# Values and row sums of two head pairs in one stretch of 32-column tiles, in an attention and GELU kernel

## The chip, the cores and the metric

The kernel runs on one core of one Trainium2 chip. The metric is the device time of one execution in microseconds (us). The engines are named as in the profile: PE is TensorE's matmul side and PEld its loading of weights, DVE is VectorE, ACT is ScalarE, POOL is GpSimd, SP is the engine that issues most DMAs.

## The reference

Cosine attention over 8 batches of 12 heads (448 positions of 64 elements), then a layer of two matrices with an exact GELU between them over all 3584 positions.

```python
q_n = q / (norm(q) + 1e-06)
k_n = k / (norm(k) + 1e-06)
scores = q_n @ k_n.transpose(0, 1, 3, 2) / tau
attn = exp(scores - max(scores))
attn = attn / (sum(attn) + 1e-09)
x = (attn @ v), heads side by side          # 3584 x 768
h = x @ w_in                                # 768 x 2048
out = (0.5 * h * (1 + erf(h / sqrt(2)))) @ w_out    # 2048 x 768
```

## The kernel before

A batch has six pairs of heads; a pair's two heads fill the 128 partitions of a tile (64 each). With normalised q and k the scores are bounded, so no maximum is subtracted. The kernel goes through the batches in turn: an attention stage `attention(b, fill)` of six intervals, then a linear stage `first(b)` with the first matrix and the GELU. The second matrix's matmuls (`second_pieces`, 128 rows by 384 columns, 16 of them to an output tile) are cut into single matmuls and put as filling, `run(n)`, between the pieces of the next attention stage. A batch pair has seven blocks of 128 rows: batches 1, 3, 5 and 7 get three blocks, which is 96 filling matmuls, and batches 2, 4 and 6 get four, which is 128. Batch 0 has its own attention code with nothing to fill in.

A pair's scores come in four chunks of 112 keys; TensorE writes a chunk for both heads, ScalarE makes exp of it:

```python
def scores(g, c0):
    qkT = qkT_t[g]
    for c in (c0, c0 + 1):
        st = ps_st.tile([128, 2, 512], F32, tag="st")        # 2 buffers
        for h in range(2):
            rows = slice(h * D, (h + 1) * D)
            nc.tensor.matmul(st[:CS, h, :S], lhsT=qkT[rows, 1, c, :], rhs=qkT[rows, 0, :, :], ...)
        pt = ptp.tile([CS, 2, S], BF16, tag="pt")            # 12 buffers
        nc.scalar.activation(pt, st[:CS, :, :S], AF.Exp, scale=inv_tau)
```

The values, the row sums and the division. `o` and `sm` have one PSUM buffer each. The sums of two pairs (four heads) are made by `sums_two` as four tiles of 32 columns side by side, turned into reciprocals on VectorE, and spread over the partitions through a DMA to memory and back; `sums_one` makes those of one pair with 64 columns each, so that they need no DMA:

```python
def values(g, copy):
    o = ps_acc.tile([128, 512], F32, tag="o")                # 1 buffer
    for c in range(NC):
        for h in range(2):
            nc.tensor.matmul(o[h * D:(h + 1) * D, :S], lhsT=v_t[g][:, h, c, :],
                             rhs=pt_t[g, c][:, h, :], start=(c == 0), stop=(c == NC - 1))
    os_t[g] = o[:, :S]
    if copy:
        os = osp.tile([128, S], F32, tag="os")
        nc.vector.tensor_copy(os, o[:, :S])
        os_t[g] = os

def sums_two(g):
    sm = ps_acc.tile([128, 512], F32, tag="sm")              # 1 buffer
    for c in range(NC):
        for j in range(2):
            for h in range(2):
                r = 32 * (2 * j + h)
                nc.tensor.matmul(sm[r:r + 32, :S], lhsT=ones[:, :32], rhs=pt_t[g + j, c][:, h, :],
                                 start=(c == 0), stop=(c == NC - 1), tile_position=(0, r))
    rs = reciprocal(g, sm)               # VectorE: transpose (tr), reciprocal (rc), transpose (rs)
    nc.sync.dma_start(out=rows[g:g + 2]..., in_=rs[0:128:32, :])
    rb = osp.tile([128, 2, S], F32, tag="rb", bufs=2)
    for h in range(2):
        nc.sync.dma_start(out=rb[h * D:(h + 1) * D], in_=rows[g:g + 2, h, :].partition_broadcast(D))
    # ... rb_t[g + j] = rb[:, j, :]; the exp tiles are dropped

def normalise(g, eng):
    eng.tensor_tensor(x_t[b][:, p, :], os_t.pop(g), rb_t.pop(g), ALU.mult)
```

The attention stage. The calls `upto(f, n)` issue the steps f of later pairs up to number n: scaling (`scale`, GpSimd) and transposing (`transposes`, DMA) of this batch's q and k, squares (GpSimd) and their sums (`reduce`, VectorE) and loads for the next:

```python
def attention(b, fill):
    # ... run(n) issues the next n filling matmuls
    tail = 12
    nxt = (b + 1) * HP
    for i in range(HP):
        g = b * HP + i
        share = (len(fill) - tail) // (HP - i)
        if i > 0:
            scores(g, 0)
        # ... roots, scale, transposes of this batch
        upto(square, nxt + min(i, 3))
        upto(reduce, nxt + min(max(i - 1, 0), 3))
        one = i == HP - 1
        if i == 0:
            run(24)
        else:
            run(share // 3)
            if one:
                sums_one(g - 1)
            values(g - 1, not one)
            if i in (2, 4):
                sums_two(g - 2)
        scores(g, 2)
        if one:
            normalise(g - 1, nc.vector)
        if i in (0, 3):
            upto(load_v, g // 3 + 3, NV)
        if i in (3, 5):
            for j in (3, 2):
                normalise(g - j, nc.gpsimd)
        if i in (3, 4):
            upto(load_qk, nxt + i + 2)
        run(share - share // 3 if i else 6)
    g = b * HP + HP - 1
    run(len(fill))
    sums_one(g)
    values(g, False)
    normalise(g, nc.vector)
```

The linear stage takes the pairs of x in the order 0, 1, 4, 2, 3 and 5 (batch 0: as they come), as pairs 2 and 3 wait for the DMA of their sums; the first scores of the next batch end it:

```python
def first(b):
    # ... for each of 16 output blocks m: 6 matmuls hp <- x, wi (128 x 448), then GELU on ScalarE
    upto(load_wo, 4)
    for n in range(nxt + 1, nxt + 4):
        upto(scale, n)
        upto(transposes, n)
    upto(load_qk, nxt + 10)
    upto(square, nxt + 6)
    upto(reduce, nxt + 6)
    # ...
    scores(nxt, 0)
```

Of the kernel before, what the change touches and what calls it, by code (L numbers as in the profile page):

```python
# [15 lines left out]
def kernel(  # L16
# [15 lines left out]
    nc = tc.nc  # L32
    B, H, S, D = q.shape
    NC = 4
    CS = S // NC
    HP = H // 2
# [52 lines left out]
    qk_t, v_t, sq_t, nq_t, rn_t, qkb_t, qkT_t, pt_t = {}, {}, {}, {}, {}, {}, {}, {}  # L89
# [96 lines left out]
# [3 lines that stand above are left out]
            st = ps_st.tile([128, 2, 512], F32, tag="st", name=f"st{g}_{c}")  # L189
            for h in range(2):  # L190
                rows = slice(h * D, (h + 1) * D)
                nc.tensor.matmul(st[:CS, h, :S], lhsT=qkT[rows, 1, c, :], rhs=qkT[rows, 0, :, :],  # L192
                                 start=True, stop=True)
            pt = ptp.tile([CS, 2, S], BF16, tag="pt", name=f"pt{g}_{c}")
            nc.scalar.activation(pt, st[:CS, :, :S], AF.Exp, scale=inv_tau)  # L195
            pt_t[g, c] = pt

    def values(g, copy):
        o = ps_acc.tile([128, 512], F32, tag="o", name=f"o{g}")
        for c in range(NC):  # L200
            for h in range(2):
                nc.tensor.matmul(o[h * D:(h + 1) * D, :S], lhsT=v_t[g][:, h, c, :],  # L202
                                 rhs=pt_t[g, c][:, h, :], start=(c == 0), stop=(c == NC - 1))
        os_t[g] = o[:, :S]
        if copy:
            os = osp.tile([128, S], F32, tag="os", name=f"os{g}")
            nc.vector.tensor_copy(os, o[:, :S])  # L207
            os_t[g] = os
        v_t.pop(g)
# [3 lines left out]
    def reciprocal(g, sm):  # L213
        tr = rcp.tile([128, S // 32, 32], F32, tag="tr", name=f"tr{g}")
        nc.vector.transpose(tr.rearrange("p b r -> p (b r)"), sm[:, :S])  # L215
        rc = rcp.tile([128, S // 32], F32, tag="rc", name=f"rc{g}")
        nc.vector.reciprocal(rc, tr[:, :, 0])
        rs = rcp.tile([128, S // 32, 32], F32, tag="rs", name=f"rs{g}")
        nc.vector.transpose(rs, rc.to_broadcast([128, S // 32, 32]))  # L219
        return rs.rearrange("p b r -> p (b r)")  # L220


    def sums_one(g):
        sm = ps_acc.tile([128, 512], F32, tag="sm", name=f"sm{g}")
        for c in range(NC):
            for h in range(2):
                nc.tensor.matmul(sm[h * D:(h + 1) * D, :S], lhsT=ones, rhs=pt_t[g, c][:, h, :],  # L227
                                 start=(c == 0), stop=(c == NC - 1))
        rb_t[g] = reciprocal(g, sm)
# [3 lines left out]
    def sums_two(g):  # L233
        sm = ps_acc.tile([128, 512], F32, tag="sm", name=f"sm{g}")
# [6 lines that stand above are left out]
        rs = reciprocal(g, sm)  # L241
        nc.sync.dma_start(out=rows[g:g + 2].rearrange("j h s -> (j h) s"), in_=rs[0:128:32, :])
        rb = osp.tile([128, 2, S], F32, tag="rb", name=f"rb{g}", bufs=2)
        for h in range(2):
            nc.sync.dma_start(out=rb[h * D:(h + 1) * D], in_=rows[g:g + 2, h, :].partition_broadcast(D))
        for j in range(2):
            rb_t[g + j] = rb[:, j, :]
            for c in range(NC):
                pt_t.pop((g + j, c))

    def normalise(g, eng):
        b, p = divmod(g, HP)
        eng.tensor_tensor(x_t[b][:, p, :], os_t.pop(g), rb_t.pop(g), ALU.mult)  # L253
# [48 lines left out]
    def upto(f, n, last=NG):  # L302
        while done.get(f, 0) < min(n, last):
            done[f] = done.get(f, 0) + 1
            f(done[f] - 1)

    def roots(n):
        upto(root, n, len(groups))
# [9 lines left out]
    def attention_first():  # L318
# [25 lines left out]
        upto(reduce, HP + 3)  # L344
        sums_one(HP - 1)
        values(HP - 1, False)
        normalise(HP - 1, nc.vector)
        upto(load_wo, 2)


    def attention(b, fill):
        fill = list(fill)

        def run(n):
            for _ in range(max(0, min(n, len(fill)))):
                fill.pop(0)()

        x_t[b] = xp.tile([128, HP, S], BF16, tag="x", name=f"x{b}")
        tail = 12
        nxt = (b + 1) * HP  # L360
        for i in range(HP):
            g = b * HP + i
            share = (len(fill) - tail) // (HP - i)
            if i > 0:
                scores(g, 0)

            if i == HP - 1:
                roots(2 * b + 7)
            upto(scale, min(g + 4, nxt))
            upto(transposes, min(g + 4, nxt))  # L370
            upto(square, nxt + min(i, 3))
            upto(reduce, nxt + min(max(i - 1, 0), 3))
            one = i == HP - 1
            if i == 0:
                run(24)
            else:
                run(share // 3)
                if one:
                    sums_one(g - 1)
                values(g - 1, not one)  # L380
                if i in (2, 4):
                    sums_two(g - 2)
            scores(g, 2)
            if one:
                normalise(g - 1, nc.vector)
            if i in (0, 3):
                upto(load_v, g // 3 + 3, NV)
            if i in (3, 5):
                for j in (3, 2):
                    normalise(g - j, nc.gpsimd)  # L390
            if i in (3, 4):
                upto(load_qk, nxt + i + 2)
            run(share - share // 3 if i else 6)
        g = b * HP + HP - 1
        run(len(fill))
        sums_one(g)
        values(g, False)
        normalise(g, nc.vector)


    def first(b):
        sb, hf = divmod(b, 2)
        if hf == 0:
            g_t[sb] = gp.tile([128, KF, 2 * S], BF16, tag="g", name=f"g{sb}")
        if b == 0:
            roots(HP + 1)
        nc.scalar.preload_act_table_set(GELU_SET)
        nxt = (b + 1) * HP
        hps = {}


        order = (0, 1, 4, 2, 3) if b else range(KD - 1)

        def mm(m, kds):
            for kd in kds:
                nc.tensor.matmul(hps[m], lhsT=wi[:, kd, m * 128:(m + 1) * 128],  # L416
                                 rhs=x_t[b][:, kd, :], start=(kd == 0), stop=(kd == KD - 1))


        for m in range(2):  # L420
            hps[m] = ps_mm.tile([128, 512], F32, tag="mm", name=f"hp{b}_{m}")[:, :S]
            mm(m, order)
        st = ps_st.tile([128, 2, 512], F32, tag="st", name=f"hp{b}_2")
        for m in range(2, 4):
            hps[m] = st[:, m - 2, :S]
            mm(m, order)
        upto(load_wo, 4)
        for n in range(nxt + 1, nxt + 4):
            upto(scale, n)
            upto(transposes, n)  # L430
        upto(load_qk, nxt + 10)
        upto(square, nxt + 6)
        upto(reduce, nxt + 6)
        for m in range(4):
            mm(m, (KD - 1,))
        for m in range(KF):
            if m > 3:
                hps[m] = ps_mm.tile([128, 512], F32, tag="mm", name=f"hp{b}_{m}")[:, :S]
                mm(m, range(KD))
            nc.scalar.activation(g_t[sb][:, m, hf * S:(hf + 1) * S], hps.pop(m), AF.Gelu)  # L440
        if b + 1 < B:
            nc.scalar.preload_act_table_set(EXP_SET)
            roots(2 * b + 8)
            scores(nxt, 0)
# [25 lines left out]
    fill = []  # L470
    for b in range(B):
        if b == 0:
            attention_first()
        else:
            attention(b, fill)
        first(b)
        sb, hf = divmod(b, 2)
        todo = [(t, ni) for t in (range(3) if hf == 0 else range(3, 7)) for ni in range(2)]
        if b == 0:
            todo.sort(key=lambda x: x[1])  # L480
        fill = [f for t, ni in todo for f in second_pieces(sb, t, ni)]
# [37 lines left out]
```

## Time and profile before

| | |
|---|---|
| time, median of three | 457.26 us (456.58 to 458.76) |
| span of the profiled execution | 456.8 us |
| TensorE busy | 443.7 us, 2912 matmuls |
| ScalarE busy | 264.7 us |
| GpSimd busy | 234.1 us |
| VectorE busy | 180.2 us |
| granted TensorE clock, mean of the span | 0.993 |
| attention stages, 96 filling matmuls (batches 1, 3, 5, 7) | 33.49, 32.24, 32.06, 32.07 us |
| attention stages, 128 filling matmuls (batches 2, 4, 6) | 36.69, 36.70, 36.70 us |

The two lower rows were read off the chain that ended last: a stage goes from the first filling matmul to the first matmul of the linear stage. A matmul's duration in the profile is that of its passage through the array, in which the next one already runs: to find what a matmul costs, take the difference between starts, not the duration. In the profile's names a line such as `o<-pt,v 112*64 112x448 bf16` is a matmul into the tile o with 112 rows and 64 columns of weights and 448 moving columns. `st` are scores, `op` is the filling (second matrix), `hp` the first matrix, `o` the values, `sm` the row sums.

### The profile page before, as it was taken

What the parts mean: (1) busy time and instruction counts of PE and PEld (TensorE: products, weight loads), DVE (VectorE), ACT (ScalarE), POOL (GpSimd) and SP (SyncE); (2) the same over time, 40 slices, a digit from 0 to 9 for tenths busy, and PEclk for the clock granted to TensorE, in tenths of its full rate; (3) what the DMA queues carried; (4) which work ended last, traced back from release to release, by engine and by line L of the source; (5) the groups of instructions that cost most, each with busy time, mean ns of one, the idle gap of its engine ahead of it and who ended that gap; (6) DMA issues with size and microseconds to landing.
All of it is one profiled execution on the core that took longest, in us unless ns stands there. A gap on an engine that the chain in (4) does not pass through costs nothing.

```text
span 456.8 us, 7314 instructions
## 1 busy us (share of the span) xinstructions
PE 443.7 (97%) x2912; PEld 216.8 (47%) x2912; DVE 180.2 (39%) x294; ACT 264.7 (58%) x380; POOL 234.1 (51%) x213
## 2 busy tenths in 40 slices
PE   7999998999999999999999999999999999999995
PEld 4444543445445554455444554445444554444563
DVE  4686316532365305443255322753054431342021
ACT  4886486636665467744767358745766357773300
POOL 3997756391934719274642928367381744121000
PEclk9899999999999999999999999999999999999998
DMA  8999999764864817757456566747185711821022
GB/s 202 238 241 207 195 209 199 199 159 113 126 145 139 198 37 128 165 132 188 61 121 177 128 160 103 148 138 188 35 131 141 181 31 19 142 84 34 1 69 70
DMA packets 87458, 61.46 MB, mean 135 GB/s; under 512 B 42312, under 2 KB 82304, under 8 KB 87424
## 3 DMA queue, kind: packets, MB, share of 16 engines
q1 hardware_dynamic: 70400, 48.97, 45.4%
q0 software_dynamic: 16784, 11.80, 17.9%
q8 instruction: 22, 0.36, 0.3%
q10 hardware_dynamic: 240, 0.23, 0.2%
q14 instruction: 12, 0.10, 0.1%
HBM read 52.04 MB, written 11.11 MB: 138 GB/s over the span
## 4 chain that ended last, share of the span: by engine, by line
PE 86%; ACT 6%; DMA 4%; POOL 1%; issue 1%; DVE 1%; SPq 0%; POOLq 0%
PE hp L416 31%; PE op L267 31%; PE st L192 9%; PE o L202 8%; ACT pt L195 5%; PE sm L227 3%; PE sm L239 2%; DMA v<-in_v_dram 2%; DMA qkT<-qkb 2%; POOL qkb L166 1%; ACT g L440 1%; PE spin L314 1%; DMA qk<-in_q_dram 1%; DVE nq L137 0%; PE tp L182 0%
## 5 line engine op out<-in xcount | busy, mean ns | idle before, releaser
L195 ACT ACTIVATE pt<-st 112x896 bf16<-112x896 f32 x192 | 164.4, 913 | 56.6 <-PE st L192 56.4
L267 PE MATMUL op<-wo,g 128*128 128x384 bf16 x896 | 160.4, 327 | 0.0
L416 PE MATMUL hp<-x,wi 128*128 128x448 bf16 x768 | 148.1, 352 | 0.5
L440 ACT ACTIVATE g<-hp 128x448 bf16<-128x448 f32 x128 | 67.0, 545 | 99.8 <-PE hp L416 99.2
L267 PEld LDWEIGHTS <-g 128*128 128x128 bf16 x896 | 80.7, 98 | 72.2 <-issue 25.0
L416 PEld LDWEIGHTS <-wi 128*128 128x128 bf16 x768 | 74.4, 98 | 73.6 <-issue 3.3
L166 POOL TENSOR_TENSOR qkb<-qk,rn 112x512 bf16<-112x512 f32 x95 | 96.8, 1046 | 7.6 <-DVE rn L157 7.4
L127 POOL TENSOR_TENSOR sq<-qk 112x1024 f32<-112x1024 f32 x44 | 82.3, 1889 | 1.7 <-DMA qk<-in_k_dram 1.6
L139 DVE TENSOR_REDUCE nq<-sq 112x16 f32<-112x1024 f32 x47 | 57.0, 1215 | 59.4 <-POOL sq L127 59.3
L253 POOL TENSOR_TENSOR x<-os,rb 128x448 bf16<-128x448 f32 x28 | 31.2, 1133 | 80.4 <-DMA rb<-rows 66.9
L192 PE MATMUL st<-qkT 64*112 64x448 bf16 x384 | 60.9, 376 | 4.3 <-ACT pt L195 1.9
L271 DVE COPY ot<-op 128x384 f32<-128x384 f32 x56 | 30.5, 545 | 85.7 <-PE op L267 85.7
L155 POOL TENSOR_SCALAR se<-sr 112x48 f32<-112x48 f32 x14 | 4.6, 327 | 84.1 <-ACT sr L154 84.1
L202 PE MATMUL o<-pt,v 112*64 112x448 bf16 x384 | 45.1, 357 | 0.4 <-DMA v<-in_v_dram 0.4
L192 PEld LDWEIGHTS <-qkT 64*112 64x112 bf16 x384 | 21.1, 125 | 42.4 <-issue 36.8
L157 DVE RECIPROCAL rn<-se 112x48 f32<-112x48 f32 (+1 forms) x20 | 7.8, 392 | 79.3 <-POOL se L155 79.0
L202 PEld LDWEIGHTS <-v 112*64 112x64 bf16 x384 | 18.9, 109 | 19.9 <-issue 9.7
L207 DVE COPY os<-o 128x448 f32<-128x448 f32 x28 | 17.5, 624 | 24.5 <-PE o L202 24.5
L215 DVE STREAM_TRANSPOSE tr<-sm 128x448 f32<-128x448 f32 x34 | 21.7, 637 | 8.4 <-PE sm L227 5.1
L219 DVE STREAM_TRANSPOSE rs<-rc 128x448 f32<-128x448 f32 x34 | 21.9, 645 | 1.2
L227 PE MATMUL sm<-pt,ones 112*64 112x448 bf16 x160 | 19.0, 359 | 0.0
L314 PE MATMUL spin<-blank,ident 112*112 112x448 bf16 x48 | 14.7, 456 | 1.3 <-POOL ident masks.py:199 1.3
(35 smaller groups left out, 124.0 us busy)
## 6 DMA issues: line engine op xcount, KB each, us to landing
qk<-in_q_dram SPq DMA_DIRECT2D x48, 224.0 KB, 4.9
qk<-in_k_dram SPq DMA_DIRECT2D x47, 224.0 KB, 5.1
rb<-rows SPq DMA_DIRECT2D x28, 224.0 KB, 4.7
v<-in_v_dram POOLq DMA_DIRECT2D x15, 336.0 KB, 5.9
wi<-in_moe_w_in_dram POOLq DMA_DIRECT2D x4, 768.0 KB, 11.6
wo<-in_moe_w_out_dram POOLq DMA_DIRECT2D x4, 768.0 KB, 18.0
out_dram<-ot SPq DMA_DIRECT2D x8, 336.0 KB
out_dram<-ot SPq DMA_DIRECT2D x8, 288.0 KB
```

What stands on the lines that cost most here:

```text
L127: nc.gpsimd.tensor_tensor(sq, t, t, ALU.mult)
L139: nc.vector.tensor_reduce(nq, sq, mybir.AxisListType.X, ALU.add)
L166: eng.tensor_tensor(qkb[:, i].rearrange("p c h d -> p h c d"), t[:, i], rn[:, i].to_broadcast([CS, 2, NC, D]), ALU.mult)
L192: nc.tensor.matmul(st[:CS, h, :S], lhsT=qkT[rows, 1, c, :], rhs=qkT[rows, 0, :, :], start=True, stop=True)
L195: nc.scalar.activation(pt, st[:CS, :, :S], AF.Exp, scale=inv_tau)
L202: nc.tensor.matmul(o[h * D:(h + 1) * D, :S], lhsT=v_t[g][:, h, c, :], rhs=pt_t[g, c][:, h, :], start=(c == 0), stop=(c == NC - 1))
L227: nc.tensor.matmul(sm[h * D:(h + 1) * D, :S], lhsT=ones, rhs=pt_t[g, c][:, h, :], start=(c == 0), stop=(c == NC - 1))
L253: eng.tensor_tensor(x_t[b][:, p, :], os_t.pop(g), rb_t.pop(g), ALU.mult)
L267: nc.tensor.matmul(ps[:, :NH], lhsT=g_t[sb][:, kf, t * 128:(t + 1) * 128], rhs=wo[:, kf, ni * NH:(ni + 1) * NH], start=(kf == 0), stop=(kf ...
L271: nc.vector.tensor_copy(ot[:, ni * NH:(ni + 1) * NH], ps[:, :NH])
L416: nc.tensor.matmul(hps[m], lhsT=wi[:, kd, m * 128:(m + 1) * 128], rhs=x_t[b][:, kd, :], start=(kd == 0), stop=(kd == KD - 1))
L440: nc.scalar.activation(g_t[sb][:, m, hf * S:(hf + 1) * S], hps.pop(m), AF.Gelu)
```

## The change

The values of the pairs 0 to 3 of a batch are computed with 32 columns of weights at a time (two matmuls for what was one), the form that the sums of two pairs have. They are held back so that two pairs' values and their four heads' sums come one after another, values, sums, values, in the intervals 2 and 4, with no matmul of another form between. The intervals 1 and 3 are left with scores and filling only, and the filling is shared out by a fixed plan in place of equal shares. The change is meant to have TensorE change its form less often. In batch 0's linear stage fewer q and k loads are issued, and the rest in the first interval of batch 1.

```diff
--- before.py
+++ after.py
@@ -197,10 +197,13 @@
 
     def values(g, copy):
         o = ps_acc.tile([128, 512], F32, tag="o", name=f"o{g}")
+        w = 32 if copy else D
         for c in range(NC):
             for h in range(2):
-                nc.tensor.matmul(o[h * D:(h + 1) * D, :S], lhsT=v_t[g][:, h, c, :],
-                                 rhs=pt_t[g, c][:, h, :], start=(c == 0), stop=(c == NC - 1))
+                for r in range(0, D, w):
+                    nc.tensor.matmul(o[h * D + r:h * D + r + w, :S], lhsT=v_t[g][:, h, c, r:r + w],
+                                     rhs=pt_t[g, c][:, h, :], start=(c == 0), stop=(c == NC - 1),
+                                     tile_position=(0, h * D + r))
         os_t[g] = o[:, :S]
         if copy:
             os = osp.tile([128, S], F32, tag="os", name=f"os{g}")
@@ -245,8 +248,6 @@
             nc.sync.dma_start(out=rb[h * D:(h + 1) * D], in_=rows[g:g + 2, h, :].partition_broadcast(D))
         for j in range(2):
             rb_t[g + j] = rb[:, j, :]
-            for c in range(NC):
-                pt_t.pop((g + j, c))
 
     def normalise(g, eng):
         b, p = divmod(g, HP)
@@ -356,11 +357,12 @@
                 fill.pop(0)()
 
         x_t[b] = xp.tile([128, HP, S], BF16, tag="x", name=f"x{b}")
-        tail = 12
         nxt = (b + 1) * HP
+
+        plan = {96: ((20, 6), (9, 9), (0, 10), (9, 9), (0, 10), (2, 12)),
+                128: ((24, 6), (14, 13), (0, 14), (14, 13), (0, 14), (4, 12))}[len(fill)]
         for i in range(HP):
             g = b * HP + i
-            share = (len(fill) - tail) // (HP - i)
             if i > 0:
                 scores(g, 0)
 
@@ -371,28 +373,29 @@
             upto(square, nxt + min(i, 3))
             upto(reduce, nxt + min(max(i - 1, 0), 3))
             one = i == HP - 1
-            if i == 0:
-                run(24)
-            else:
-                run(share // 3)
-                if one:
-                    sums_one(g - 1)
-                values(g - 1, not one)
-                if i in (2, 4):
-                    sums_two(g - 2)
+            run(plan[i][0])
+            if one:
+                sums_one(g - 1)
+                values(g - 1, False)
+            elif i in (2, 4):
+
+                values(g - 2, True)
+                sums_two(g - 2)
+                values(g - 1, True)
             scores(g, 2)
             if one:
                 normalise(g - 1, nc.vector)
             if i in (0, 3):
                 upto(load_v, g // 3 + 3, NV)
+            if b == 1 and i == 0:
+                upto(load_qk, nxt + 4)
             if i in (3, 5):
                 for j in (3, 2):
                     normalise(g - j, nc.gpsimd)
             if i in (3, 4):
                 upto(load_qk, nxt + i + 2)
-            run(share - share // 3 if i else 6)
+            run(plan[i][1])
         g = b * HP + HP - 1
-        run(len(fill))
         sums_one(g)
         values(g, False)
         normalise(g, nc.vector)
@@ -428,7 +431,7 @@
         for n in range(nxt + 1, nxt + 4):
             upto(scale, n)
             upto(transposes, n)
-        upto(load_qk, nxt + 10)
+        upto(load_qk, nxt + (10 if b else 7))
         upto(square, nxt + 6)
         upto(reduce, nxt + 6)
         for m in range(4):
```

## The prediction

> **What bounds the kernel now.** I read the page's busy shares and its chain first, then TensorE's timeline in an attention stage with a long and one with a short filling, then VectorE's and GpSimd's timelines beside them, last the waits and a table by stage. The page:
>
> ```profile
> PE 443.7 (97%) x2912; PEld 216.8 (47%) x2912; DVE 180.2 (39%) x294; ACT 264.7 (58%) x380; POOL 234.1 (51%) x213
> PE 86%; ACT 6%; DMA 4%; POOL 1%; issue 1%; DVE 1%; SPq 0%; POOLq 0%
> ```
>
> TensorE is busy for 97% of the span and is 86% of the chain that ended last. No other engine can be the bound over the whole; only what shortens TensorE's own sequence, or its few waits, is worth anything. Busy time hides how well TensorE is used, so I read start times. Batch 2 (128 filling matmuls), TensorE's timeline; columns are start, duration, engine, line, operation, tiles, shapes, count:
>
> ```profile
> 116.31 0.40 PE L192 MATMUL st<-qkT 64*112 64x448 bf16 x2
> ...
> 117.26 0.99 PE L267 MATMUL op<-wo,g 128*128 128x384 bf16 x5
> 118.17 0.95 PE L202 MATMUL o<-pt,v 112*64 112x448 bf16 x8
> 119.05 0.58 PE L192 MATMUL st<-qkT 64*112 64x448 bf16 x4
> 119.57 2.12 PE L267 MATMUL op<-wo,g 128*128 128x384 bf16 x12
> 121.62 0.59 PE L192 MATMUL st<-qkT 64*112 64x448 bf16 x4
> 122.14 0.99 PE L267 MATMUL op<-wo,g 128*128 128x384 bf16 x5
> 123.06 0.95 PE L202 MATMUL o<-pt,v 112*64 112x448 bf16 x8
> 123.93 0.94 PE L239 MATMUL sm<-pt,ones 112*32 112x448 bf16 x16
> 124.81 0.58 PE L192 MATMUL st<-qkT 64*112 64x448 bf16 x4
> ```
>
> Take differences of starts, not durations. Twelve op cost 2.05 us (119.57 to 121.62), five cost 0.92: so 0.1625 a matmul and **0.10 for the stretch itself**. st: 0.52 for four matmuls, two at a time. o: 0.88 for eight, two at a time. sm: 0.88 (I use 0.87 from other batches) for sixteen, **four at a time**. In batch 3, where sums and values of one pair both use 64 columns, sm and o together take 191.51 to 193.14, 1.63: 8 more matmuls than o alone for 0.75, so a round costs 0.1875 and a stretch 0.13. Every change of matmul form costs 0.10 to 0.13.
>
> Batch 3 (96 filling matmuls) shows a wait in the same rows, where the filling is too short:
>
> ```profile
> 182.44 0.95 PE L202 MATMUL o<-pt,v 112*64 112x448 bf16 x8
> 183.32 0.86 PE L192 MATMUL st<-qkT 64*112 64x448 bf16 x4
> 184.11 1.47 PE L267 MATMUL op<-wo,g 128*128 128x384 bf16 x8
> ```
>
> This st takes 0.79 to the next stretch and not 0.52: its second chunk waits for a score buffer that ScalarE's exp (1.72 us for two chunks) has not freed. Over batch 3 such excesses are 0.27 + 0.26 + 0.10 + 0.10 = 0.73. The waits of TensorE, with the one large one, are:
>
> ```profile
> PE st L192 <- ACT pt L195: 1.9, 8, 0.4
> ...
> PE st L192 <- DMA qkT<-qkb: 1.5, 1, 1.5
> ```
>
> The second is in batch 1 (74.56 us), whose stage, first here, is longer than the like one (batch 3, second); the third line is batch 4, with 128 filling matmuls. Columns: stretch, length, busy time of PE, PEld, DVE, ACT, POOL, clock, DMA share, GB/s:
>
> ```profile
> 58.28:91.77 33.49, 31.75 (x237) 14.73 (x238) 15.54 (x27) 24.13 (x31) 18.02 (x17) 1.00 1.03 204
> ...
> 166.48:198.72 32.24, 31.90 (x238) 14.75 (x238) 15.63 (x27) 24.14 (x31) 17.53 (x17) 1.00 0.62 127
> 217.81:254.51 36.70, 36.48 (x271) 17.39 (x270) 16.86 (x29) 24.14 (x31) 18.90 (x18) 1.00 0.56 122
> ```
>
> **What the Trainium skill says.** *TensorEngine Tiling (Array Packing)*, Key Properties: changing the tiling mode, not just the tile, drains TensorE. The trace agrees: 0.10 to 0.13 us at each change of form, about none from sm to o where both have 64 columns. *TensorE: Matmul & The Clock Gate*, Part 3, "Measured speedup vs the span model": matmuls in different column tiles run beside one another. The trace agrees: 16 of 32 columns take the 0.87 us of 8 of 64. The same page, Part 1, "Architectural detail", calls VectorE a strict FIFO, so a copy out of PSUM stands behind whatever was issued before it; in batch 3's VectorE timeline no later instruction passes a waiting one. *PSUM — Partial Sum Buffer*, "PSUM bank collisions raise a hardware error": a bank must be guarded between the matmul and its reader. There is one bank named o, so this decides the cost below.
>
> **The change part by part.**
>
> *Fewer stretches.* Two intervals of batch 3 now: four st 2.08, four op stretches with 22 matmuls 0.40 + 3.575, two o 1.76, one sm 0.87; sum 8.69. After: four st 2.08, three op stretches with 28 matmuls 0.30 + 4.55, one stretch of 12 rounds of four (o 4, sm 4, o 4) 12 x 0.1875 + 0.13 = 2.38; sum 9.31. Six filling matmuls more, moved here from the first and last interval where they shorten an existing stretch, are 0.975: like for like 8.34. Saved 0.35, twice a batch, in seven batches: **4.9 us**. Doubling the values' instructions costs no rounds, if their tiles go like sm's.
>
> *A new wait.* The second values write the one bank o, from which VectorE must first have copied the first values. Batch 2's VectorE:
>
> ```profile
> 124.05 0.62 DVE L207 COPY os<-o 128x448 f32<-128x448 f32 x1 [0.97 <-PE o L202]
> 124.93 0.65 DVE L215 STREAM_TRANSPOSE tr<-sm 128x448 f32<-128x448 f32 x1 [0.26 <-PE sm L239]
> ```
>
> The copy starts 0.99 after its first matmul (123.06) and takes 0.62; early in the trace TensorE follows VectorE 0.06 after a copy's end. So o is free at 1.67 after the stretch's start; eight rounds are done at 1.50. Wait 0.17, fourteen times: **2.4 us lost**.
>
> *ScalarE gets its time.* In the short batches the distance from one st to the next was 1.93 to 1.99 us; after, it is 0.52 + nine op 1.56 = 2.08, 0.52 + 2.55 = 3.1 or 0.52 + ten op 1.73 = 2.25, against 1.74 for two exps. The excesses of the middle intervals go: 0.73 in batch 3; batches 5 and 7 are 0.17 shorter than batch 3, so 0.55 there and I take 0.55 for each of four: **2.2 us**. What stays is the short distance after the op stretch of six, in both kernels (116.31 to 117.26).
>
> *Batch 1.* The diff leaves three pairs' q and k loads out of the first linear stage, where the DMA share is over 1.2, and issues them after the transposes of batch 1's first interval. The transposes of its fourth pair, issued at 66.88 now, stood behind those loads; GpSimd finished their input at about 63.4. So they go some 3 us sooner, and the 1.46 wait ends: **1.4 us**.
>
> *The path of the sums' reciprocals.* In the short batches GpSimd scales pairs 2 and 3 just before the linear stage needs them:
>
> ```profile
> 197.23 2.23 POOL L253 TENSOR_TENSOR x<-os,rb 128x448 bf16<-128x448 f32 x2 [3.74 <-DMA rb<-rows]
> ```
>
> From the start of sm to the end of the broadcast row's last VectorE step is 2.6 us, the DMA then takes 6.6 to 7.1 (four short batches), the two multiplies 2.2. After: 0.75 (sm's place in the stretch) + 2.6 + 6.9 + 2.25 = 12.5 after the stretch's start. TensorE reaches pair 3 of the linear stage at 2.55 + 0.52 + 1.73 + 0.52 + 0.43 + 1.63 + 0.52 + 2.05 + 1.63 + 0.77 = 12.35. So about 0.15 more waiting in each short batch, **0.6 us lost**; in the long batches four more op (0.65) and two more in the last interval (0.33) cover it.
>
> Sum: 4.9 - 2.4 + 2.2 + 1.4 - 0.6 = 5.5 us less, 451.8. I round to **452.0**, as the losses are likelier to be too small than the gains.
>
> **The rivals.** *VectorE is late.* If another VectorE instruction stands ahead of the copy, the wait in the stretch is not 0.17 but up to 1.2 more, the length of the reduction (L139), which waits for GpSimd's squares in that very interval. Fourteen times 1.2 is 17 us: 472, slower. For it: in batch 3 GpSimd's first square ended at 176.24 and the reduction ran 176.27 to 177.49, and the stretch would start at about 176.9. Against it: the copy is due only 0.99 later, at 177.9; the interval before the second stretch has no copy left, so VectorE has caught up. It is a margin of 0.4, and in batch 1 I expect to lose some 0.3. *The 32-column values don't run four at a time*, for they share moving data two by two: eight more rounds in each of 14 stretches, 21 us, 476. Sums of the same shapes speak against it. *The batch 1 wait only moves* to the next pair's transposes, which then stand behind the loads: 1.4 less, 453.4. *The linear stage waits* for the reciprocals in earnest, 0.5 in each short batch: 1.4 less again, 453.2.
>
> **Range and chances.** No wait in the stretches and all of ScalarE's 0.73: about 2.4 + 0.7 better, 448.7. Wait 0.35, batch 1's wait moved and linear stages waiting: 2.5 + 1.4 + 1.4 worse, 457. Eight in ten: 449.0 to 456.0. Faster by over 2% needs under 448.1, which takes nearly every gain and no loss: 0.07. Slower by over 2% needs over 466.4, one of the first two rivals in full: 0.03. Within 2%: 0.90.
>
> **What would show it.** Each step has its row in the changed profile: 12 rounds of four in 2.5 to 2.6 us from first values to st, with a wait of TensorE on VectorE's os of about 0.17 each; no st longer than 0.52 in the middle intervals; batch 1's stage like batch 3's, at about 31.1, from 33.5 and 32.2; the long stages at 36.3, from 36.7; the fifth linear matmul (pair 3) waiting 0.1 to 0.4 in short batches. I am wrong if waits on os are near 1 us, if a round of values takes twice 0.19, or if transposes stop TensorE for over 1 us anywhere.

## The result and the profile after

The changed kernel takes 453.02 us (median; 452.40 to 453.88) against 457.83 us of the kernel before beside it: a ratio of 0.9898, 95% interval 0.9866 to 0.9930. Predicted were 452.0 us, with a range of 449.0 to 456.0.

The page of the changed kernel, busy shares and then the chain that ended last, by engine:

```profile
PE 437.3 (97%) x3136; PEld 218.8 (49%) x3136; DVE 178.5 (40%) x294; ACT 265.1 (59%) x380; POOL 234.3 (52%) x213
...
PE 83%; DMA 5%; POOL 4%; ACT 3%; DVE 2%; issue 1%; SPq 1%; POOLq 0%
```

There are 224 matmuls more (the halved values), and TensorE is busy 6.4 us less. It is as full as before, with a shorter sequence. ScalarE's part of the chain has halved (6% to 3%); GpSimd's, VectorE's and the DMA's have grown. Where they stand in it is shown under batch 1 below.

TensorE's timeline in batch 2, from the end of interval 1 (counted from 0) through the values and sums of interval 2 (start, duration, engine, line, operation, tiles, shapes, count); `op` is now L268, `o` L204, `sm` L242:

```profile
118.65 2.29 PE L268 MATMUL op<-wo,g 128*128 128x384 bf16 x13
120.86 0.59 PE L192 MATMUL st<-qkT 64*112 64x448 bf16 x4
121.38 0.94 PE L204 MATMUL o<-pt,v 112*32 112x448 bf16 x16
122.15 0.93 PE L242 MATMUL sm<-pt,ones 112*32 112x448 bf16 x16
123.05 0.94 PE L204 MATMUL o<-pt,v 112*32 112x448 bf16 x16
123.92 0.59 PE L192 MATMUL st<-qkT 64*112 64x448 bf16 x4
```

Again by starts: first values 0.77, sums 0.90, second values 0.87; from 121.38 to 123.92 it is 2.54 us. The first values cost no change of form on leaving (0.77, where o alone took 0.88). The sums take 0.90 and not 0.75, though four rounds are the same work. The missing 0.15 is a wait for VectorE that the profile does not list as one; VectorE's rows of the same time show it:

```profile
122.37 0.62 DVE L210 COPY os<-o 128x448 f32<-128x448 f32 x1 [1.18 <-PE o L204]
123.13 0.65 DVE L218 STREAM_TRANSPOSE tr<-sm 128x448 f32<-128x448 f32 x1
```

The copy of the first values ends at 122.99, and the second values start 0.06 later. Thirteen of the fourteen stretches of values, sums, values took 2.54 us. The attention stages of batches 1, 3 and 4 (from and to, length, busy time of PE, PEld, DVE, ACT, POOL, clock, DMA share, GB/s):

```profile
57.23:89.55 32.32, 31.10 (x271) 15.24 (x269) 15.27 (x26) 24.32 (x31) 17.02 (x16) 1.00 1.04 200
...
164.53:195.65 31.12, 31.09 (x270) 15.18 (x268) 15.29 (x26) 24.31 (x31) 17.75 (x17) 1.00 0.61 131
214.66:250.98 36.32, 36.10 (x303) 17.84 (x301) 16.52 (x28) 24.20 (x31) 18.17 (x17) 1.00 0.56 123
```

Batch 3 stands for the short stages: it fell from 32.24 to 31.12 us. The long ones fell from 36.70 to 36.32; both are as foreseen. Batch 1 fell from 33.49 to 32.32, where 31.1 was foreseen. TensorE's waits that are new or changed (us in all, times, longest):

```profile
PE st L192 <- ACT pt L195: 1.3, 5, 0.4
PE o L204 <- DVE os L210: 1.2, 1, 1.2
PE o L204 <- DVE rs L222: 1.0, 1, 1.0
PE hp L419 <- POOL x L254: 0.5, 1, 0.5
```

The wait for the transposes (1.5 us) is gone from the list. The last three lines are new, once each. The third is in batch 0, whose attention the change leaves alike; **the second and the fourth are in batch 1**. TensorE's stretch there, then VectorE:

```profile
68.06 0.93 PE L242 MATMUL sm<-pt,ones 112*32 112x448 bf16 x16
70.17 0.94 PE L204 MATMUL o<-pt,v 112*32 112x448 bf16 x16 [1.17 <-DVE os L210]
```

```profile
68.36 1.22 DVE L139 TENSOR_REDUCE nq<-sq 112x16 f32<-112x1024 f32 x1 [3.49 <-POOL sq L127]
69.50 0.61 DVE L210 COPY os<-o 128x448 f32<-128x448 f32 x1
```

From sums to second values it is 2.11 us and not 0.90. The copy was due at about 68.3 and stood behind a reduction that had waited for GpSimd's squares, and these for the load of k (1.20 us idle before the squares). This is what has come into the chain (start, length, what):

```profile
54.67 11.61 DMA qk<-in_k_dram
66.44 1.90 POOL sq L127
68.36 1.22 DVE nq L139
69.58 0.54 DVE os L210
```

The profiles' spans differ by more than the medians, 5.9 against 4.8 us. 0.97 of it lies before the first linear stage, in batch 0's attention, whose instructions the change leaves alike; over the profiles of all kernels here it took 37.2 to 39.4 us to get there.

### The profile page after: what moved, and what is told of

It is laid out like the page before. It is cut to its first block, busy times and chain, and to the rows that moved or that the text cites. A ratio compares the mean times of both kernels' runs of the same rounds, so it can differ in the third digit from the quotient of the medians.

```text
span 450.9 us, 7780 instructions
## 1 busy us (share of the span) xinstructions
PE 437.3 (97%) x3136; PEld 218.8 (49%) x3136; DVE 178.5 (40%) x294; ACT 265.1 (59%) x380; POOL 234.3 (52%) x213
## 4 chain that ended last, share of the span: by engine, by line
PE 83%; DMA 5%; POOL 4%; ACT 3%; DVE 2%; issue 1%; SPq 1%; POOLq 0%
PE op L268 31%; PE hp L419 28%; PE st L192 10%; PE o L204 8%; DMA qk<-in_k_dram 3%; PE sm L230 3%; PE sm L242 2%; POOL qkb L166 2%; ACT pt L195 2%; POOL sq L127 2%; ACT g L443 1%; DMA qk<-in_q_dram 1%; DVE nq L139 1%; PE spin L315 1%; DMA rows<-rs 1%
## 5 line engine op out<-in xcount | busy, mean ns | idle before, releaser
L268 PE MATMUL op<-wo,g 128*128 128x384 bf16 x896 | 157.9, 327 | 0.0
L268 PEld LDWEIGHTS <-g 128*128 128x128 bf16 x896 | 81.9, 98 | 70.6 <-issue 21.6
L254 POOL TENSOR_TENSOR x<-os,rb 128x448 bf16<-128x448 f32 x28 | 31.3, 1137 | 68.3 <-DMA rb<-rows 65.5
L192 PE MATMUL st<-qkT 64*112 64x448 bf16 x384 | 59.4, 373 | 1.7 <-ACT pt L195 1.3
L204 PE MATMUL o<-pt,v 112*32 112x448 bf16 (+1 forms) x608 | 44.9, 354 | 2.2 <-DVE os L210 1.2
L204 PEld LDWEIGHTS <-v 112*32 112x32 bf16 (+1 forms) x608 | 19.8, 99 | 21.1 <-issue 9.2
L112 POOL DMA_DIRECT2D v<-in_v_dram x17 | 14.0, 823 | 0.0
```

The costliest lines, as they stand in the source:

```text
L204: nc.tensor.matmul(o[h * D + r:h * D + r + w, :S], lhsT=v_t[g][:, h, c, r:r + w], rhs=pt_t[g, c][:, h, :], start=(c == 0), stop=(c == NC - 1),
L268: nc.tensor.matmul(ps[:, :NH], lhsT=g_t[sb][:, kf, t * 128:(t + 1) * 128], rhs=wo[:, kf, ni * NH:(ni + 1) * NH], start=(kf == 0), stop=(kf ...
```

## The experiments

Lengths of stages and stretches are taken from each kernel's timeline. "Short" stages have 96 filling matmuls, "long" ones 128. Ratios are to the kernel before on the same chip.

**Values of 64 columns in the new order.**

```diff
-        w = 32 if copy else D
+        w = D
```

> The changed kernel with the values back at 64 columns of weights; order, plan and loads stay changed. My theory (each change of form costs 0.1 to 0.13 us, the narrow form is worth only the two changes it saves less the 0.15 us wait it uncovers): the stretch of values, sums, values goes from 2.54 to 2.63 us, with no wait of TensorE on VectorE's copy, as the sums now take until after the copy; 14 times 0.09, about +1.2 us, 454.2 us; stages of 96 filling matmuls 31.3 us, of 128 36.5 us. Rival (the narrow form is where the gain comes from): back to near the kernel before, over 456 us. Rival (narrow values run slower than wide ones): faster than 453 us.

Measured: 455.99 us, ratio 0.9959 (0.9943 to 0.9976). Stretches 0.88 + 0.87 + 0.88 = 2.63 us, with no wait but in batch 1; short stages 31.29, long ones 36.48. The stages lengthened as expected, by 0.16, so for the stages both rivals fall. Of the 0.38 us that a long stage gained, 0.22 are there with wide values too and come from having fewer stretches of filling; the narrow form is worth 0.16, or 0.09 a stretch. The time lengthened by 2.8 us and not 1.2, which is about where the first rival expected it. But of the 2.9 us between this profile's span and the changed kernel's, the stages make up 0.9. Another 1.2 lies before the first linear stage (39.42 against 38.23), in instructions that the edit leaves alike, and 0.8 in the linear stages of batches 3 and 7, which waited 0.18 and 0.65 us for pairs 2 and 3, as those of the changed kernel did not. Whether the waits belong to the wide form or to the scatter of that DMA path isn't separated.

**Sums before both values.**

```diff
-                values(g - 2, True)
                 sums_two(g - 2)
+                values(g - 2, True)
                 values(g - 1, True)
```

> The changed kernel with the order sums, values, values in the stretch. My theory (the second values wait for VectorE's copy out of the one buffer o, free 1.65 us after the first values begin): nothing stands between the two values any more, so the wait grows from 0.15 to about 0.9 us and the stretch from 2.54 to 3.30 us; thirteen times 0.75 and once 0.1 (batch 1's first stretch, which waits longer already): about +9.9 us, 463 us. Rival (the 0.15 us between the sums and the second values is a cost of going from one tile to another and no wait for the copy): the order makes no difference, 453 us.

Measured: 473.76 us, ratio 1.0356 (1.0325 to 1.0387). The wait is one for the copy, as the theory had it, but twice as long as I expected. TensorE in batch 4, then VectorE:

```profile
236.10 0.94 PE L242 MATMUL sm<-pt,ones 112*32 112x448 bf16 x16
236.87 0.93 PE L204 MATMUL o<-pt,v 112*32 112x448 bf16 x16
239.26 0.94 PE L204 MATMUL o<-pt,v 112*32 112x448 bf16 x16 [1.46 <-DVE os L210]
```

```profile
237.10 0.65 DVE L218 STREAM_TRANSPOSE tr<-sm 128x448 f32<-128x448 f32 x1 [1.18 <-PE sm L242]
...
238.63 0.58 DVE L210 COPY os<-o 128x448 f32<-128x448 f32 x1
```

I had forgotten that the new order holds for VectorE too: the reciprocal of the sums (237.10 to 238.63) now comes before the copy. The stretch takes 4.03 us (236.10 to 240.13) in place of 2.54: fourteen times 1.49 is 20.9, and 453.0 + 20.9 = 473.9. **The order values, sums, values is what makes the one buffer o bearable.**

**Copying half of o.**

```diff
-            nc.vector.tensor_copy(os, o[:, :S])
+            nc.vector.tensor_copy(os, o[:, :S // 2])    # os has S // 2 columns
 ...
+            for s in (slice(0, n), slice(n, S)):        # n = S // 2, on GpSimd
+                eng.tensor_tensor(x_t[b][:, p, s], os, rb[:, s], ALU.mult)
```

> The changed kernel with VectorE copying only half of the columns of o (the first half of each pair's values is used for both halves, so half of the values of pairs 0 to 3 is left out; GpSimd multiplies twice 224 columns). My theory (the 0.15 us after the sums is the wait for this copy, 0.62 us long): a copy of half the length is done before the sums are, the wait goes, a stretch takes 2.39 us, fourteen times 0.15 is 2.1 us: 450.9 us, or up to 0.5 us more where the linear stage then waits. Rival (a cost of passing from sums to values): stretches stay at 2.54 us.

Measured: 454.57 us, ratio 0.9898 (0.9865 to 0.9930). TensorE in batch 4:

```profile
231.17 0.93 PE L242 MATMUL sm<-pt,ones 112*32 112x448 bf16 x16
231.93 0.93 PE L204 MATMUL o<-pt,v 112*32 112x448 bf16 x16
```

The sums take 0.76, so the 0.15 is the wait for the copy. Short stages fell to 30.81, long ones to 36.00, yet the time didn't fall: the linear stages of batches 3 and 5 now waited 0.38 us each for pairs 2 and 3, and that of batch 1 was 5.0 us longer than one without waits. GpSimd's doubled multiplies, which this kernel added, can have a small part in that (2.5 us for a batch's two pairs, in place of 2.2); in batch 1 the way of the row sums through memory took 10.1 us, in place of 7.4. In this profile, what the stretch gave, the linear stages took. The execution profiled took longest of six (455.35 us; the shortest took 452.02), so batch 1 need not lose as much in the others.

**The new sharing-out alone, on the kernel before.**

```diff
+        plan = {96: ((20, 6), (3, 9), (3, 9), (3, 9), (3, 9), (3, 19)),
+                128: ((24, 6), (5, 12), (5, 12), (5, 12), (5, 12), (6, 24))}[len(fill)]
 ...
```

> The kernel before, its values and sums untouched and in every interval, with only the filling of the 96-matmul batches shared out otherwise: 20 and 6 in the first interval, 3 and 9 in the next four, 3 and 19 in the last. As many stretches as before. My theory (ScalarE's exps stop TensorE in the short batches because scores follow each other too soon there): the delays of the scores in the middle intervals go, and the stages of batches 1, 3, 5, 7 fall by 0.4 to 0.7 us, to about 31.5 us (batch 1 to 33.1 us); in all about -2.1 us, 455.7 us. Rival (the delays are no matter of spacing, only fewer stretches shorten the stage): 457.8 us, stages of 32.06 us as before.

Measured: 457.59 us, ratio 0.9993 (0.9979 to 1.0006). The stages did what was expected (31.87, 31.60, 31.59; batch 1 33.20), 1.6 us together, and no gain is shown in the time. In its profile the linear stage of batch 3 waited 1.0 us for pairs 2 and 3, 0.9 more than before. Hence the next.

**The same, with the linear stage in another order** (`early` for each of the first four blocks, then `rest`).

```diff
-        order = (0, 1, 4, 2, 3) if b else range(KD - 1)
+        early, rest = ((0, 1, 4), (2, 3)) if b else (range(KD - 1), ())
 ...
```

> The kernel before with the filling shared out otherwise (as in the earlier run of that plan) and with the linear stage running pairs 0, 1, 4 of its first four blocks before pairs 2 and 3 of any, which puts 1.7 us more work ahead of pair 3. My theory (the time that the new plan freed in the short batches was lost again where the linear stage waited for pairs 2 and 3): no linear stage waits any more, short stages stay at about 31.6 us, and the ratio to the kernel before goes from 0.9993 to about 0.996. Rival (the plan frees nothing that lasts): ratio 0.999.

Measured: 456.06 us, ratio 0.9957 (0.9939 to 0.9976). Stages as in the run before this one but for batch 1 (33.50), every linear stage 19.01 us. So the sharing-out's gain shows together with the split linear stage and not without it. What the new order alone gives the kernel before wasn't run; in that kernel's profile it could save only 0.09 and 0.10 us, the waits of batches 3 and 7.

**That order on the changed kernel.**

> The changed kernel with the linear stage running pairs 0, 1, 4 of its first four blocks before pairs 2 and 3 of any; nothing else. My theory (in the changed kernel pairs 2 and 3 come within 0.5 us of when the linear stage needs them in the short batches, and too late in batch 1): batch 1's linear stage falls from 19.65 to 19.01 us and the occasional waits of the others go; ratio from 0.9898 to about 0.988. Rival (the wait moves to pair 5 or the next attention stage): 0.990.

Measured: 451.91 us, ratio 0.9873 (0.9848 to 0.9899). All linear stages 19.01 us. The interval overlaps that of the changed kernel, so a gain isn't shown; and batch 1's attention stage took 34.67 us in this profile, with a copy still later.

**The loads put back.**

```diff
-            if b == 1 and i == 0:
-                upto(load_qk, nxt + 4)
 ...
-        upto(load_qk, nxt + (10 if b else 7))
+        upto(load_qk, nxt + 10)
```

> The changed kernel with the q and k loads where they were (four pairs in batch 0's linear stage). My theory: the wait for the transposes of batch 1's fourth pair comes back with about 1.4 us, the wait for VectorE's copy in batch 1's first stretch (1.36 us beyond the usual) stays or grows as the squares wait for the same loads; stage of batch 1 about 33.5 us against 32.3 us, in all about +1.2 us, 454.2 us. Rival (the deferral only moves the wait from the transposes to the copy): batch 1's stage stays at 32.3 us and the time at 453 us.

Measured: 453.68 us, ratio 0.9902 (0.9879 to 0.9924), no difference to the changed kernel. Batch 1's stage 32.52 us, its linear stage 19.85. There was no wait for the transposes: the stretch before them waited 1.27 us for the copy, and by then they had landed.

**The reduction after the stretch**, and the same with the loads put back.

```diff
-            upto(reduce, nxt + min(max(i - 1, 0), 3))
             one = i == HP - 1
 ...
                 values(g - 1, True)
+            upto(reduce, nxt + min(max(i - 1, 0), 3))
             scores(g, 2)
```

> The changed kernel with VectorE's reduction of the next batch's squares issued after the stretch of values and sums in place of before it. My theory (VectorE takes its work in order, so that in batch 1's first stretch the copy out of o stood behind a reduction that waited for a late load): the 1.36 us beyond the usual wait in that stretch goes, all fourteen stretches take 2.54 us, batch 1's stage falls from 32.3 to about 31.0 us and the time by 1.3 us, to 451.7 us. Rival (batch 1 is held up by its loads in any case): the wait turns up at the transposes of a later pair or in the linear stage, and the time stays at 453 us.

> The changed kernel with the reduction after the stretch as in the run beside it, and the q and k loads where they were before the change. My theory (the loads delay the transposes of batch 1's fourth pair; with the early reduction that wait was hidden under the wait for the copy): with the copy no longer late, TensorE reaches the fourth pair some 1.4 us sooner and waits for its transposes there by about as much; batch 1's stage 32.5 us as with the loads put back alone, time 453.5 us. Rival (the deferred loads have no effect at all): as the run beside it, 31.0 us and 451.7 us.

Measured: 454.06 us, ratio 0.9897 (0.9858 to 0.9937), and 453.41 us, ratio 0.9882 (0.9855 to 0.9909). In both, all fourteen stretches took 2.54 us, so the copy's lateness was the reduction's doing. But the time didn't move. With the loads late, TensorE stopped at the scores of batch 1's **fifth** pair:

```profile
77.12 0.58 PE L192 MATMUL st<-qkT 64*112 64x448 bf16 x4 [1.81 <-DMA qkT<-qkb]
```

With the loads early, at those of the **fourth**, as in the kernel before:

```profile
73.93 0.59 PE L192 MATMUL st<-qkT 64*112 64x448 bf16 x4 [1.10 <-DMA qkT<-qkb]
```

Then batch 1's linear stage waited for pairs 2 and 3, 2.1 us in the first run and 1.7 us in the second. Of the first run's two accounts, the rival that batch 1 is held up in any case is the one that stands; the second run came out as its theory had it (453.5 us).

**Versions meant to beat both.** The first has the reduction after the stretch, the split linear stage, and 22 and 7 (long: 24 and 7) filling matmuls in the first interval, the second interval at 8 and 8 in the short batches, and 1 less before the last sums. The second keeps the changed plan in the short batches. The third is the second with the loads put back.

> A version that should beat both: reduction after the stretch; first interval 22 and 7 (24 and 7) filling matmuls in place of 20 and 6 (24 and 6), taken from the second (short batches) and last interval; the linear stage runs pairs 0, 1, 4 of its first four blocks before pairs 2 and 3 of any. My theory: batch 1's stretch -1.36 us, its linear stage's wait of 0.65 us gone, the scores' delays in the first intervals 0.3 us less in four and 0.2 us less in three batches: 3.7 us together, 449.3 us, short stages 30.8 us, no linear stage waiting for pairs 2 or 3. Rival (the delays are ScalarE's work that only moves): short stages stay at 31.1 us and the time is 451 us.

> The earlier best version without its new plan for the short batches, which did nothing (31.23 us against 31.13 us): linear stage split, reduction after the stretch, 24 and 7 in place of 24 and 6 matmuls in the long batches. Short stages 31.1 us, long ones 36.15 us; ratio 0.984 as the earlier one, if batch 1's transposes come in time; up to 0.988 if the wait for those of its fifth pair shows, as it did (1.8 us) with the reduction moved alone.

> The version beside it with the q and k loads where they were before the change. If deferring the loads only chooses which pair's transposes TensorE waits for in batch 1 (the fourth with the loads early, the fifth with them late): a wait of about 1.1 us at the fourth pair and a ratio within 0.002 of the run beside it. If deferring them is of use: slower by over 1 us.

Measured: 451.00 us, ratio 0.9840 (0.9805 to 0.9874); 451.35 us, 0.9853 (0.9824 to 0.9881); 451.45 us, 0.9848 (0.9827 to 0.9870). All three beat the kernel before by about 1.5%. Their intervals overlap, so none is shown to be ahead of another, and each overlaps the changed kernel's by a little, so that they beat it isn't shown either. One matmul more in the first interval took 0.17 us off each long stage (36.15). Two and one matmuls more in the first interval of the short batches took nothing off the stages of batches 3 and 5 (31.23, in place of 31.12), which is what the first one's rival said, and 0.05 off batch 7's. The first one's ratio leaves out one execution of 457.39 us, which counts as one in a slower state of the chip. Batch 1 went differently in each: stage and linear stage took 50.2, 52.7 and 51.4 us, the third with 1.2 us of waiting at the fourth pair. Deferring the loads is of no use that could be measured, here as in the changed kernel.

## Why the prediction was right, step by step

**Fewer stretches, less the wait for the copy: 4.9 - 2.4 = 2.5 us predicted.** Right. The three long stages, in which nothing else changed, give it alone: 0.38 each, so 0.19 a stretch and 2.7 over fourteen. The wait measured 0.15 and not 0.17, and the run with half a copy showed that it is that wait.

**ScalarE gets its time: 2.2 us.** Right in size for the changed kernel. The distances from scores to the next stretch, beyond 0.52, summed to 0.90, 1.17, 1.00 and 1.00 us in the four short batches and now to 0.42 to 0.44: 2.3 together. The sharing-out alone shortened the same stages, but its gain shows in the time only with the split linear stage.

**Batch 1: 1.4 us, because its transposes no longer stand behind the loads.** This step failed: it took the end of that one wait for a gain. SP's queue, before and after (the first row holds the transposes of two later pairs as well):

```profile
66.88 7.54 SPq L176 DMA_TRANSPOSE qkT<-qkb  x3
62.41 1.23 SPq L176 DMA_TRANSPOSE qkT<-qkb  x1
```

The transposes did go earlier, and their wait ended. But it ended just as well with the loads put back, while the copy came late. With the copy in time, one order of loads made TensorE wait for the fourth pair, the other for the fifth. In the changed kernel the 1.46 us came back as 1.2 us of waiting for the copy, 0.3 left. The prediction had named both rivals, a late VectorE with "some 0.3" in batch 1 and a wait that only moves to the next pair, and gave them too little; the 0.3 isn't in its sum. It did not ask when the load behind the squares lands. That was 9.21 us after the stage's start, and 9.27 with the other loads put back: deferring them didn't bring it sooner.

**The reciprocals' path: 0.6 us lost, 0.15 in each short batch.** The sum was nearly right, its place was not. Batches 3, 5 and 7 didn't wait (0.09 and 0.10 us in 3 and 7 before), as the DMA took 6.3 to 6.7 us there and not 6.9; batch 1 waited 0.64, as it took 7.4. Together 0.45 lost.

**The sum.** 2.7 + 2.3 + 0.3 - 0.5 = 4.8 us, with 4.8 between the medians. The prediction's own sum was 5.5: batch 1 gave 1.1 less, and the other three steps 0.4 more together. That the number came out nearer than its worst step is luck, as the errors partly cancelled. The other half of the distance from 452.0 to 453.02 is that the kernel before took 457.83 beside the changed one, and 457.26 when the prediction was made.

Of the rivals, 32-column values at half speed can be excluded (sixteen of them took 0.77 us), and a late VectorE in all stretches too. (The prediction's 472 and 476 us for the two are 3 us too high: 452.0 with its 17 and 21 us more is 469 and 473.) But the late VectorE was much nearer than the margin of 0.4 us by which the prediction set it aside. In the profile of the changed kernel the reduction ended within 0.04 us of the time when the copy was due in five of the fourteen stretches: the first of batches 3 and 5 (in batch 3 at 175.60, with the copy starting at 175.58) and the second of batches 2, 4 and 6. That it cost nothing there was luck, which the version with the reduction after the stretch doesn't need. The linear stage waiting in earnest was not the changed kernel's case, but in their profiles it took back all that half the copy had gained in the stages, and 0.9 of the 1.6 us of the sharing-out alone.

What stays open: which of its waits batch 1 falls into, and how much it loses, differed between kernels that differ elsewhere, and each was profiled once; several of the profiles (half the copy, the split order on the changed kernel, the late reduction with the loads put back, the second of the last three) are of the longest of their kernel's executions. The DMA share in the changed kernel is 1.28 to 1.33 from 40 to 70 us; that this traffic is the cause isn't shown, as a run with less of it was not made.

## What to carry to other kernels

When TensorE is full, count its changes of form, as a stretch of one form cost 0.10 to 0.13 us beyond its rounds here: put matmuls of one form together even if that needs more instructions, and look then for the buffer that the next of them must share. In such a stretch place work that does not need the buffer between its two users, and issue nothing ahead of the copy that may itself have to wait (here that ended a wait of 1.2 us, though batch 1 then waited elsewhere). Read a gain in a stage against the next stage's waits before counting it: a transfer that was just hidden takes back what was freed.

## What the runs showed of the hardware that was not expected

The way of a row sum from VectorE through memory to GpSimd's multiply took, after the second sums of batches 2 to 7, 6.2 to 7.5 us in most cases and 7.95 at most; in batch 1, 6.4 to 11.0 us. So a slack of under 1.5 us on this path was none. And the time up to the first linear stage varied by 2.2 us between profiles with the same instructions in it, more than most of the effects studied here: stages had to be compared, and not spans.
